# Storing x^T by blocks of three tiles instead of tile by tile, with new order numbers, in a fused attention and softplus-MLP kernel

## The chip, the cores and the metric

The kernel runs on one core of a Trainium2 chip. The metric is the device time of one execution in microseconds (us). A profile is one such execution, recorded by the hardware profiler; its span runs from the first to the last instruction.

## What is computed

The reference takes q, k and v (8 batches, 8 heads, 576 rows, 64 columns), a gain g_norm and two weights. Linear attention, a root-mean-square norm per head, and a two-layer MLP with a softplus between follow:

```python
kv  = np.einsum('bhsd,bhse->bhde', k, v)
out = np.einsum('bhsd,bhde->bhse', q, kv)
x   = out / sqrt(mean(out * out, axis=-1) + 1e-6) * g_norm     # 4608 rows of 512 after the heads are joined
h   = x @ w_in                                                  # 512 x 2048
y   = (maximum(h, 0) + log1p(exp(-abs(h)))) @ w_out             # 2048 x 512
```

The weights come as 64-bit floats and are put together from their words on the core; each factor of the MLP is split into parts (three for x and the weights), so a product is several TensorE passes.

## The kernel before

**Tiles, blocks and phases.** The 4608 rows of x are 36 tiles of 128 rows (P). Three tiles (TB) make a block of 384 rows (NT); there are 12 blocks. The 2048 hidden columns are 16 chunks of 128. The MLP goes in three phases over the chunks (`ENDS`): in phase 0 blocks 0 to 3 take four chunks each and the others six, in phases 1 and 2 the rest. One pair of block and chunk is a step, 192 in all. A step (`step`, lines 647 to 695) is twelve matmuls of x with w_in (L660, 128x384), softplus and its splitting on ScalarE (L682, L684) and VectorE (L671, L675), and nine matmuls with w_out (L667). At a phase's end the partial sums go to DRAM (L724) and come back in the next (L707).

**The attention part** (`rows`, from line 508) makes one tile of x after the other. q is turned, by TensorE (L577) and a copy on ScalarE (L584) for batches 0 and 1, by VectorE (L552) for the later ones, whose q is loaded by `load_q` in eight transfers a batch. TensorE multiplies with kv (L521) into one of two PSUM slots `o`. ScalarE squares (L590), VectorE sums by head (L525), GpSimd takes the root (L528, L529), VectorE multiplies (L533). `kv_of` loads k and v (L491, and L489 for the last rows of a batch) and forms kv on TensorE (L502) in a PSUM slot: s0 or s1 for the first two batches, the single slot `tp` for the rest.

**x^T.** The MLP needs x turned. For the first twelve tiles (`BY_PE`) TensorE turns it (`turn_x`, L539) into a PSUM slot `xp`: the slot `tp` for tiles 0 to 5 (`AT_ONCE`), an `o` slot for tiles 6 to 11. Tiles 0 to 5 are split straight from PSUM for phase 0 (`split`, L445 on ScalarE, L448 and L452 on VectorE). All twelve are also copied by ScalarE (L599) into a slot of ring m, and stored into the DRAM array xd (L600), 256 KB a tile, in rows of 128 floats (512 bytes). Tiles from 12 on are turned by VectorE (L616) into the buffer xb, and a block of three is stored by four transfers (L620). `x_again` (L635) loads a tile of x^T back, again in rows of 512 bytes (L638), in phase 0 for tiles from 6 on and in the later phases for all, and splits it; it waits for the stores listed in `x_there`.

**Weights.** `weight` loads a chunk of w_in or w_out (L283, 512 KB) into one of two raw slots, puts the floats together (L294 to L324) and `divide` splits them (L356 to L378).

**Order.** Every operation is a task with an engine, a cost in ns, the tasks it follows, the slots it takes (`take`) and gives back (`give`), and a position `pos`. The planner (`Plan.order`, line 69) runs through a simulated time when the kernel is built: among tasks of an engine that could start within 150 ns of one another, the lowest `pos` goes first. A task whose slot is not free is passed over. A task with a `size` books the transfer engines for so many ns, and its end is 2000 ns later. The order is fixed by that; on the chip each engine takes its instructions in it, and each waits for what it needs. SyncE (SP) issues nearly all transfers, in order. Ring m has 13 slots (four of them kept from loads), xb and tp have one, o has two. Where TensorE has time free early on, the planner puts in spare matmuls of the identity (`warm`, L778), up to the seventh step.

**Positions.** The list P0 gives them: CONVERT when the first four chunks' factors are converted, FETCH when they are loaded, EARLY the attention part's offsets, LATER the other chunks' factors. EARLY[0] and [1] set the tiles of block 0: tile t stands at `t * EARLY[0] + EARLY[1]`. EARLY[5] sets kv of batch 0 ahead of tile 0, EARLY[9] and [10] how far ahead of their use the loads of x^T and of partial sums are listed.

Of the kernel before, what the change touches and what calls it, by code (L numbers as in the profile page):

```python
# [18 lines left out]
P = 128  # L19
# [21 lines left out]
class Plan:  # L41
# [15 lines left out]
    def slot(self, ring):  # L57
        return Slot(ring)

    def add(self, engine, ns, run, after=(), pos=0.0, take=(), give=(), size=0, behind=None, follows=None):  # L60
        t = Task(engine, ns, run, [a for a in after if a is not None], pos, list(take), list(give), size)
        for s in t.give:
            s.readers += 1
        self.tasks.append(t)
        t.follows = follows
        t.behind = behind
        return t
# [79 lines left out]
def kernel(  # L147
# [24 lines left out]
    nc = tc.nc  # L172
# [5 lines left out]
    KD, KF = d_model // P, d_ff // P  # L178
    NT = 384
    TB = NT // P  # L180
# [6 lines left out]
    PLACES = 8  # L187
    LAST = PHASES[-1]

    P0 = [-72.5, -3.2, -24.8, -9.7, -19.6, 1.5, -23.9, 2.2, -63.0, -49.3, -55.7, -21.2, -38.7, -7.7,  # L190
          -2.7, -4.7, 2.0, -26.5, 14.0, 10.5, 5.5, 17.5, -2.0, 2.5, 3.5, 21.5, -35.0, 10.0, 6.5, 41.0,
          51.0, 65.5, 53.5, 72.5, 90.5, 95.5, 114.5, 109.5, 111.5, 8.5]
    CONVERT, FETCH, EARLY, LATER = P0[:8], P0[8:16], P0[16:27], P0[27:]
    BY_PE = 12
    AT_ONCE = 2 * TB
# [27 lines left out]
    slot, add = plan.slot, plan.add  # L223

    def new(s, shape, dtype=F32):
        if s.ring == "o":
            s.tile = o_banks[:, :, s.place]
            return s.tile
        pool = ps if s.ring in PS else sb
        s.tile = pool.tile(shape, dtype, tag=f"{s.ring}_{s.place}", name=f"{s.ring}_{s.place}")  # L230
        return s.tile
# [172 lines left out]
    xd = [dram.tile([d_model, NT], F32, name=f"x{n}") for n in range(n_blocks)]  # L404
    xb_slots = {}
    x_there = {}
# [26 lines left out]
    def split(ph, t, x, ready, pos):  # L433
        n, i = divmod(t, TB)
        if i == 0:
            xv_slots[ph, n] = slot("xv")
        dst = xv_slots[ph, n]

        def cols(m, dtype=F32):
            if dst.tile is None:  # L440
                new(dst, [P, 3, KD, NT], F32R)
            return (dst.tile if dtype == F32R else dst.tile.bitcast(F32))[:, m, :, i * P:(i + 1) * P]

        def high():
            nc.scalar.activation(cols(0, F32R), x.tile, func=AF.Identity, scale=g_down)  # L445

        def low():
            nc.vector.scalar_tensor_tensor(out=cols(1, F32R), in0=x.tile, scalar=g_col, in1=cols(0),  # L448
                                           op0=ALU.mult, op1=ALU.subtract)

        def less():
            nc.vector.scalar_tensor_tensor(out=cols(2, F32R), in0=cols(1), scalar=-RADIX, in1=cols(0),  # L452
                                           op0=ALU.mult, op1=ALU.add)

        before = x_split.get((ph, n), [None])[-1:]
        a = add("ACT", 700, high, [ready] + ([] if i == 0 else [first_high[ph, n]]), pos, [dst] if i == 0 else [])
        if i == 0:
            first_high[ph, n] = a
        b = add("DVE", 740, low, [a], pos, [], [x])
        c = add("DVE", 700, less, [b], pos)  # L460
        x_split.setdefault((ph, n), []).append(c)
# [6 lines left out]
    def x_pos(t):  # L468

        n = t // TB  # L470
        return t * EARLY[0] + EARLY[1] if n == 0 else first_step[0, n] - (EARLY[2] if n == 1 else EARLY[3]) + t % TB
# [35 lines left out]

    def rows(t):
        pos = x_pos(t)
        tp, qT, o, x, r, xp, xg = (slot(n) for n in ("tp", "m", "o", "x", "r", "tp" if t < AT_ONCE else "o", "m"))  # L510

        def out_rows():

# [27 lines left out]
        def part_of_qT(n, r0):  # L541
            if qT.tile is None:
                new(qT, [P, NP, P])
            return qT.tile[:, :, r0:r0 + n]

        turned = []
        for b, r0, n, s0 in parts(t):
            if b >= 2:
                if b not in q_slots:
# [3 lines left out]
                        out=part_of_qT(n, r0),  # L553
                        in_=q_slots[b].tile.rearrange("k (p s) -> k p s", p=NP)[:, :, s0:s0 + n]),
# [24 lines left out]
            tp = turn_q.__defaults__[-1]  # L579
# [3 lines left out]
            a = add("PE", 440, turn_q, [ld], pos - 1, [tp], [q_s])  # L583
# [3 lines left out]
        a = o_task = add("PE", 640, out_rows, turned + need, pos, [o], [qT])  # L587
        for pt in parts(t):
            o_tasks.setdefault(pt[0], []).append(a)
        a = add("ACT", 600, lambda: nc.scalar.activation(new(x, [P, H, D]).rearrange("s (a k) d -> s a (k d)", k=2), o.tile, func=AF.Square,  # L590
                                                              scale=D ** -0.5), [a], pos, [x])
        a = add("DVE", 690, reduce, [a], pos, [r])
        a = add("POOL", 2300, root, [a], pos)
        a = add("DVE", 700, norm, [a, o_task], pos, [], [o, r])
        if t < BY_PE:
            a = add("PE", 440, turn_x, [a], pos + 0.5, [xp], [x])
            if t < AT_ONCE:
                split(0, t, xp, a, pos + 0.5)
            a = add("ACT", 600, lambda: nc.scalar.copy(new(xg, [P, KD, P]), xp.tile), [a], pos + 1, [xg], [xp])  # L599
            x_there[t] = [add("SP", 450, lambda: nc.sync.dma_start(  # L600
                out=x_of(t), in_=xg.tile), [a], pos + 1, [], [xg], 1000)]
            return


# [1 line left out]
        n, i = divmod(t, TB)  # L606
        g = TB if n < n_blocks - 1 else 1
        i0, i = i - i % g, i % g
        if i == 0:
            xb_slots[n] = slot("xb"), []  # L610
        xb, turns = xb_slots[n]
# [18 lines left out]
    def x_of(t):  # L630

        n, i = divmod(t, TB)
        return xd[n][:, i * P:(i + 1) * P].rearrange("(a p) t -> p a t", p=P)
# [120 lines left out]
    for c in range(KF):  # L754
        for j in (2 * c, 2 * c + 1):
            pos = CONVERT[j] if c < 4 else LATER[c - 4] + LATER[12] * (j % 2)
            weight(j, pos, FETCH[j] if c < 4 else pos)
    for b in range(B):
        kv_of(b)
        for t in range(n_tiles):  # L760
            if parts(t)[-1][0] == b:
                rows(t)
# [51 lines left out]
```

## Time and profile before

| | |
|---|---|
| three runs | 908.24, 908.87, 909.06 us |
| median | 908.87 us |
| the profiled execution | 908.87 us |
| its span | 907.1 us |
| mean granted TensorE clock | 0.996 |
| first product of the MLP (L660) starts | 39.67 us |
| last product (L667) ends | 903.2 us |
| the twelve stores of x^T (L600) are issued | 29.4 to 95.4 us |
| bytes moved | 131.59 MB in 211,835 packets |

A row of groups has the line, the engine, the operation, its output and input tiles, its shape and count, then busy us, the mean ns of one, and the idle time of the engine ahead of it with what ended it. "PEld" is the load of the stationary operand, "SPq" the queue of SyncE. In the line of slices each digit is the busy share of a fortieth of the span (22.7 us) in tenths, 9 being 90% or more.

### The profile page before, as it was taken

How to read it: one execution, taken by the hardware profiler on the slowest of the kernel's cores; microseconds unless marked ns; L12 is line 12 of the kernel's file. 1: busy time of each engine (PE TensorE's matmuls, PEld its weight loads, DVE VectorE, ACT ScalarE, POOL GpSimd, SP SyncE). 2: the span in 40 equal slices, each digit the busy share in tenths (PEclk: the TensorE clock that was granted, in tenths of full speed). 3: DMA queues.
4: the chain of work that ended last, by engine and by line, in shares of the span. 5: the costliest groups of instructions: out<-in, count | busy, mean ns of one | idle time of the engine just before them, and what ended most of it. 6: DMA issues, size and time to landing. Idle time of an engine off the chain costs nothing.

```text
span 907.1 us, 15612 instructions
## 1 busy us (share of the span) xinstructions
PE 894.2 (99%) x5984; PEld 789.1 (87%) x5984; DVE 624.6 (69%) x1054; ACT 409.9 (45%) x788; POOL 82.8 (9%) x79
## 2 busy tenths in 40 slices
PE   7999999999999999999999999999999999999998
PEld 5777888888888899998998999989999998999987
DVE  6977988676577877788677778886534555555553
ACT  4766555343444556644445444554323333333331
POOL 0433322122213200000000000000000000000000
PEclk8999999999999999999999999999999999999999
DMA  9999988579672626355344446550330433433323
GB/s 245 267 210 281 249 172 227 134 164 182 188 152 50 161 94 186 105 187 162 105 128 128 139 148 182 194 187 22 105 103 2 140 105 88 122 105 104 105 71 105
DMA packets 211835, 131.59 MB, mean 145 GB/s; under 512 B 102704, under 2 KB 185648, under 8 KB 211760
## 3 DMA queue, kind: packets, MB, share of 16 engines
q1 hardware_dynamic: 211600, 130.59, 52.8%
q8 instruction: 47, 0.77, 0.4%
q14 instruction: 28, 0.23, 0.1%
q10 hardware_dynamic: 160, 0.00, 0.0%
HBM read 91.75 MB, written 38.80 MB: 144 GB/s over the span
## 4 chain that ended last, share of the span: by engine, by line
PE 95%; DMA 3%; ACT 1%; DVE 0%; issue 0%; SPq 0%
PE h L660 44%; PE s L667 44%; DMA m<-in_v_dram 2%; PE o_banks L521 2%; PE tp L502 2%; PE h L778 1%; PE s L502 1%; PE tp L577 0%; DMA x<-m 0%; ACT m L599 0%; DVE xv L448 0%; PE tp L539 0%; PE o_banks L539 0%; PE h L374 0%; ACT m L584 0%
## 5 line engine op out<-in xcount | busy, mean ns | idle before, releaser
L660 PE MATMUL h<-xv,w 128*128 128x384 f32 x2304 | 434.8, 337 | 0.2 <-ACT w L378 0.2
L667 PE MATMUL s<-w,gv 128*128 128x512 f32 x1728 | 433.9, 395 | 0.0
L660 PEld LDWEIGHTS h<-xv,w 128*128 128x128 f32 x2304 | 406.4, 188 | 16.4 <-ACT w L378 0.7
L667 PEld LDWEIGHTS s<-w,gv 128*128 128x128 f32 x1728 | 319.6, 188 | 60.8 <-DVE gv L675 0.2
L682 ACT ACTIVATE g<-h 128x384 f32<-128x384 f32 x192 | 94.4, 492 | 399.2 <-PE h L660 397.1
L671 DVE TENSOR_TENSOR gv<-g,gv 128x384 fp32r<-128x384 f32 x192 | 106.5, 555 | 174.5 <-ACT gv L684 173.7
L684 ACT ACTIVATE gv<-g 128x384 fp32r<-128x384 f32 x192 | 100.8, 525 | 27.9 <-PE s L667 19.7
L675 DVE SCALAR_TENSOR_TENSOR gv<-gv 128x384 fp32r<-128x384 f32 x192 | 106.7, 556 | 5.6
L448 DVE SCALAR_TENSOR_TENSOR xv<-m,g_col,xv 128x512 fp32r<-128x512 f32 x102 | 75.9, 744 | 0.6 <-ACT xv L445 0.6
L452 DVE SCALAR_TENSOR_TENSOR xv<-xv 128x512 fp32r<-128x512 f32 x108 | 74.3, 688 | 2.7
L445 ACT ACTIVATE xv<-m,g_down 128x512 fp32r<-128x512 f32 x102 | 70.1, 711 | 2.2 <-DMA m<-x 2.0
L529 POOL TENSOR_TENSOR r<-r,half 128x8 f32<-128x8 f32 x36 | 65.3, 1813 | 3.0
L709 DVE SCALAR_TENSOR_TENSOR m<-s,scale,m 128x512 f32<-128x512 f32 x24 | 17.9, 746 | 29.7 <-PE s L667 29.7
L528 POOL TENSOR_SCALAR r<-r 128x8 f32<-128x8 f32 x36 | 16.5, 459 | 219.1 <-DVE r L525 218.6
L533 DVE TENSOR_TENSOR x<-o_banks,r 128x512 f32<-128x512 f32 x36 | 24.8, 688 | 15.3 <-POOL r L529 10.1
L709 DVE SCALAR_TENSOR_TENSOR m<-s,m 128x512 f32<-128x512 f32 x36 | 23.8, 685 | 12.4 <-PE s L667 12.3
L359 DVE TENSOR_TENSOR m<-m,w 128x512 f32<-128x512 f32 x30 | 20.5, 687 | 14.2 <-ACT w L356 14.1
L521 PEld LDWEIGHTS o_banks<-kv,m 64*64 64x64 f32 x1152 | 19.9, 134 | 10.7 <-issue 4.7
L311 ACT ACTIVATE sq<-sq,big 128x512 bf16<-128x512 bf16 x32 | 22.9, 716 | 11.0 <-DVE m L307 11.0
L525 DVE TENSOR_REDUCE r<-x 128x8 f32<-128x512 f32 x36 | 24.3, 679 | 5.0 <-ACT x L590 4.7
L521 PE MATMUL o_banks<-kv,m 64*64 64x64 f32 x1152 | 24.6, 224 | 1.2 <-ACT m L584 0.7
L590 ACT ACTIVATE x<-o_banks 128x512 f32<-128x512 f32 x36 | 21.2, 594 | 7.6 <-PE o_banks L521 3.9
(71 smaller groups left out, 429.1 us busy)
## 6 DMA issues: line engine op xcount, KB each, us to landing
m<-x SPq DMA_DIRECT2D x102, 256.0 KB, 4.7
part<-m SPq DMA_DIRECT2D x72, 256.0 KB, 2.3
m<-part SPq DMA_DIRECT2D x72, 256.0 KB, 4.0
raw<-in_moe_w_in_dram SPq DMA_DIRECT2D x16, 512.0 KB, 5.7
m<-in_k_dram SPq DMA_DIRECT2D x32, 256.0 KB, 4.8
m<-in_v_dram SPq DMA_DIRECT2D x32, 256.0 KB, 4.6
raw<-in_moe_w_out_dram SPq DMA_DIRECT2D x16, 512.0 KB, 5.5
qa<-in_q_dram SPq DMA_DIRECT2D x48, 144.0 KB, 4.7
```

Of the source, the lines that this page charges most:

```text
L445: nc.scalar.activation(cols(0, F32R), x.tile, func=AF.Identity, scale=g_down)
L448: nc.vector.scalar_tensor_tensor(out=cols(1, F32R), in0=x.tile, scalar=g_col, in1=cols(0), op0=ALU.mult, op1=ALU.subtract)
L452: nc.vector.scalar_tensor_tensor(out=cols(2, F32R), in0=cols(1), scalar=-RADIX, in1=cols(0), op0=ALU.mult, op1=ALU.add)
L521: nc.tensor.matmul(y[r0:r0 + P // 2, a, c0:c0 + D], lhsT=qT.tile[e * D:(e + 1) * D, p, r0:r0 + P // 2], rhs=kvs[b % 2][e * D:(e + 1) * D, ...
L529: nc.gpsimd.tensor_tensor(out=r.tile, in0=r.tile, in1=half, op=ALU.pow)
L660: nc.tensor.matmul(hp, lhsT=w_in.tile[:, i, kd * P:(kd + 1) * P], rhs=xv.tile[:, i, kd], start=(m == 0), stop=(m == 3 * KD - 1))
L667: nc.tensor.matmul(mine[i].tile, lhsT=gv.tile[:, m, i * P:(i + 1) * P], rhs=w_out.tile[:, m], start=(c == cs[0] and m == 0), stop=(c == cs ...
L671: nc.vector.tensor_tensor(out=gv.tile[:, 1], in0=g.tile, in1=gv.tile.bitcast(F32)[:, 0], op=ALU.subtract)
L675: nc.vector.scalar_tensor_tensor(out=gv.tile[:, 2], in0=f32[:, 1], scalar=-RADIX, in1=f32[:, 0], op0=ALU.mult, op1=ALU.add)
L682: a = add("ACT", 490, lambda: nc.scalar.activation(new(g, [P, NT]), h.tile, func=AF.Softplus, scale=1.0 + E), [a], s, [g], [h])
L684: a = add("ACT", 530, lambda: nc.scalar.activation(new(gv, [P, 3, NT], F32R)[:, 0], g.tile, func=AF.Copy, scale=DOWN), [a], s, [gv])
L709: a = add("DVE", 700, lambda: nc.vector.scalar_tensor_tensor(out=new(ot, [P, d_model]), in0=bank.tile, scalar=(scale if ph == LAST else 1. ...
```

## The change

The numbers of P0 differ, and the tail of `rows` for the first twelve tiles: ScalarE copies a tile not into a slot of ring m of its own but into its third of a block's buffer xb, the single buffer that blocks 4 to 11 use. The first tile of a block takes xb; the third is followed by one transfer of the whole block, 768 KB, whose rows are 384 floats (1536 bytes) on both sides, and whose end gives xb back. `x_there` of all three tiles is that one store. The three copies are kept in the order of the tiles' lines (`follows`). In `load_q` nothing differs: it had eight transfers a batch before.

```diff
-    P0 = [-72.5, -3.2, -24.8, -9.7, -19.6, 1.5, -23.9, 2.2, -63.0, -49.3, -55.7, -21.2, -38.7, -7.7,
-          -2.7, -4.7, 2.0, -26.5, 14.0, 10.5, 5.5, 17.5, -2.0, 2.5, 3.5, 21.5, -35.0, 10.0, 6.5, 41.0,
-          51.0, 65.5, 53.5, 72.5, 90.5, 95.5, 114.5, 109.5, 111.5, 8.5]
+    P0 = [-74.0, 0.3, -15.3, -11.7, -11.1, 1.5, -22.9, 2.2, -78.5, -42.8, -76.2, -17.2, -26.2, -5.2,
+          -0.2, -4.2, 1.5, -19.5, 14.0, 10.5, 5.5, 25.5, -2.0, 2.5, 3.5, 2.5, -45.5, 7.5, 6.5, 38.5,
+          52.0, 65.5, 54.5, 72.5, 91.0, 94.5, 114.5, 110.5, 111.0, 8.5]
     CONVERT, FETCH, EARLY, LATER = P0[:8], P0[8:16], P0[16:27], P0[27:]
...
-            a = add("ACT", 600, lambda: nc.scalar.copy(new(xg, [P, KD, P]), xp.tile), [a], pos + 1, [xg], [xp])
-            x_there[t] = [add("SP", 450, lambda: nc.sync.dma_start(
-                out=x_of(t), in_=xg.tile), [a], pos + 1, [], [xg], 1000)]
+
+            n, i = divmod(t, TB)
+            if i == 0:
+                xb_slots[n] = slot("xb"), []
+            xb, turns = xb_slots[n]
+
+            def copy():
+                if i == 0:
+                    new(xb, [P, KD, NT])
+                nc.scalar.copy(xb.tile[:, :, i * P:(i + 1) * P], xp.tile)
+
+            turns.append(add("ACT", 600, copy, [a], pos + 1, [] if i else [xb], [xp], follows=turns[-1] if turns else None))
+            if i == TB - 1:
+                st = add("SP", 450, lambda: nc.sync.dma_start(
+                    out=xd[n].rearrange("(a p) t -> p a t", p=P), in_=xb.tile), turns, pos + 1, [], [xb], 2280)
+                for u in range(t - i, t + 1):
+                    x_there[u] = [st]
             return
```

More of the change, by code (lines that the diff above doesn't have):

```diff
@@ L509, in rows @@
         pos = x_pos(t)
-        tp, qT, o, x, r, xp, xg = (slot(n) for n in ("tp", "m", "o", "x", "r", "tp" if t < AT_ONCE else "o", "m"))
+        tp, qT, o, x, r, xp = (slot(n) for n in ("tp", "m", "o", "x", "r", "tp" if t < AT_ONCE else "o"))
         def out_rows():
```

## The prediction

> **What bounds the kernel now.** I read the page first: busy shares and slices, then TensorE's order of work, then the chain of waits, then what the DMA engines do in the stretch where TensorE loses time.
>
> ```profile
> span 907.1 us, 15612 instructions
> ...
> PE 894.2 (99%) x5984; PEld 789.1 (87%) x5984; DVE 624.6 (69%) x1054; ACT 409.9 (45%) x788; POOL 82.8 (9%) x79
> ...
> PE   7999999999999999999999999999999999999998
> ...
> DMA  9999988579672626355344446550330433433323
> ```
>
> TensorE is the bound: busy 894.2 of 907.1 us. But busy is not useful. The groups of TensorE hold the spare matmuls of L778, which only fill gaps:
>
> ```profile
> L778 PE MATMUL h<-ident_r 128*128 128x512 f32 x54 | 20.4, 497 | 1.6 <-DVE ident_r L746 1.6
> ...
> L502 PE MATMUL s<-m,m 128*64 128x64 f32 x128 | 6.4, 250 | 4.3 <-DMA m<-in_v_dram 4.1
> ```
>
> So 20.4 us of spare work and 12.9 us idle (907.1 less 894.2) are all that any change of order or transfers can win; the other 874 us are products that the change leaves alone. TensorE's timeline shows where they lie (start, length, idle before it):
>
> ```profile
> 1.61 4.76 PE L778 MATMUL h<-ident_r 128*128 128x512 f32 x12 [1.61 <-DVE ident_r L746]
> ...
> 39.67 2.35 PE L660 MATMUL h<-xv,w 128*128 128x384 f32 x12
> ...
> 57.72 1.06 PE L778 MATMUL h<-ident_r 128*128 128x512 f32 x3
> ...
> 66.43 0.69 PE L502 MATMUL tp<-m,m 128*64 128x64 f32 x16 [0.94 <-DMA m<-in_v_dram]
> ```
>
> The first step's product starts at 39.67. Behind it only seven spare matmuls stand (0.40 + 1.06 + 0.71 + 0.40 = 2.6 us) and idle times of 0.21, 0.22, 0.94, 0.42 and 0.31 (2.1 us): 4.7 us lost between 39.67 and 90. Some 3.9 us of idle time are the end of the span, after the last product. The rest, about 24 us, is lost ahead of 39.67. From 90 to 903 TensorE doesn't wait at all.
>
> In that first stretch the transfers set the pace. A table by stretch (TensorE, weight loads, VectorE, ScalarE, GpSimd, granted clock, DMA share, GB/s) reads:
>
> ```profile
> 20.00:30.00 10.00, 9.48 (x166) 6.68 (x162) 9.05 (x16) 8.63 (x18) 4.32 (x4) 1.00 1.00 275
> ...
> 70.00:80.00 10.00, 9.58 (x119) 7.38 (x117) 8.00 (x14) 6.32 (x12) 1.96 (x3) 1.00 1.12 315
> ...
> 200.00:300.00 100.00, 100.00 (x934) 86.33 (x934) 65.12 (x111) 42.53 (x82) 22.64 (x20) 1.00 0.66 152
> ```
>
> DMA is at 0.9 to 1.1 up to 100 us, and VectorE at about 9 of 10 from 20 to 60: two near-bounds at once. Later DMA has a third of its time free, so a saved transfer there is worth nothing.
>
> **The stores (lines 599 to 601).** Twelve stores of 256 KB become four of 768 KB.
>
> ```profile
> L600 SPq DMA_DIRECT2D x<-m x12: 360/374/734, 29.4 to 95.4; - x12
> ...
> DMA to landing us min/median/max: 2.5/4.6/6.6
> ```
>
> All twelve lie in the saturated stretch. *Packets.* In the trace's packet records a 512-byte packet takes 28 to 32 ns in the stretches up to 100 us, a 1024-byte one 53 to 56, a 2048-byte one 87 to 92. The trace before has no 1536-byte packet: not under 54 ns, not over three of 29 (87 ns); I take 73, the middle of the rows for 1024 and 2048, which stand on both sides. A block is now 1536 packets x 29 / 16 engines = 2.78 us and becomes 512 x 73 / 16 = 2.34: 0.45 us saved (0 to 1.05), 1.8 us for four blocks (0 to 4.2). Block 3's store comes at about 95, when TensorE no longer loses time, so 1.35 us of it count (0 to 3.2). It can only eat into the 4.7 us lost after 39.67, whose largest pieces wait for loads (the value tiles at 66.43; w_in of the fourth chunk, which lands at 52.30 and holds the fourth step until 61.93). I take it whole: **-1.4 us**.
>
> The Trainium skill has a rule that speaks against this term: "DMA: Bandwidth & Descriptors", section "Specifications", has transfers from 512 bytes on at line rate, so that longer rows would win nothing. This trace differs: 512 bytes in 29 ns are 17.7 bytes per ns, 2048 in 92 are 22.3. By the page the term would be 0 and the forecast 908.0.
>
> *SP.* Eight issues fewer, 8 x 0.374 = 3.0 us of SP's time. At nothing: transfers land 4 to 7 us after their issue though each needs about 1 us of the engines, so SP is ahead by a backlog. SP's waits for the copies (6.7 us in six waits, the longest 2.4) are under that backlog too. If it were gone, each wait would stop the loads behind it, up to 2.4 us.
>
> **The ring m.** Each of the twelve copies held one of 13 slots from copy to landing, about 0.6 + 4.6 + 0.4 us; 12 x 5.6 = 67 slot-us over 70 us, so one slot in 13 comes free. The trace shows once what it cost: ScalarE's L599 waits 0.86 us at 88.15 for an earlier store, and the chain of waits runs through it. I take half, **-0.4 us** (0 to -0.9).
>
> **The numbers P0.** No transfer or instruction is added, all are re-ordered. Up to 22 us the loads keep their sequence: the same two factors first, then batch 0 of k and v, w_out of chunk 0 when a raw slot is free, then q. What moves is conversion: w_in of chunk 1 (-24.8 to -15.3) falls behind the first three tiles (-26.5, -24.5, -22.5 become -19.5, -18.0, -16.5). Tile 2's norm (L533) starts at 35.53 although GpSimd had finished at 34.42, its reduction at 31.10 although ScalarE had finished at 29.57: 1.1 + 1.5 us. But the instructions in front of both are mostly the splits and the norm of tiles 0 and 1, not conversions, so little of it can go: gain up to 2.6, loss up to the price of the second rival below (4). I take **-0.5**, near the gain that the rows leave. The retimed loads of x^T and partial sums (21.5 to 2.5, -35.0 to -45.5) matter only after the steps they are tied to; DMA's free third from 200 us on hides them, and without that cover one late load costs a TensorE step's wait of 1 to 2 us.
>
> **The wait that is added.** A block's x^T can only be stored after its third copy, and the next block can only be copied when xb is free. Reads: block 2's third copy ends at 79.6. A tile's store there landed in 3.7 us; two more tiles' worth of data (2 x 0.8) make it 5.3: 84.9. The reads then land at about 89 to 91.4, the last split (0.71 + 0.75 + 0.69) ends at about 94. Before it ended at 94.2, and the ninth step's product began at 96.7: margin 2.4 us, so **0**. If the block store takes the longest landing, 6.6 + 1.6 = 8.2 us, 0.5 us is lost. Block 3: reads from 99.5 instead of 95.9, step 12 at 115.5 against a last split at 112.2; behind the third rows that margin is 3.3 against 3.6 us of delay, 0.3 us at worst. Queued behind a waiting read on SP are k and v of later batches, whose products have no due time that TensorE misses there.
>
> **Sum.** -1.4 - 0.4 - 0.5 = -2.3. The profiled execution took 908.87 us, 1.8 us more than its span, and is the median of the three runs itself: 908.9 - 2.3 = **906.6**.
>
> **Rivals.** *First, slower: the single buffer xb.* Look at the copies of tiles 6 and 5 on ScalarE, and the first turn into xb on VectorE:
>
> ```profile
> 66.02 0.58 ACT L599 COPY m<-o_banks 128x512 f32<-128x512 f32 x1
> ...
> 70.45 0.58 ACT L599 COPY m<-tp 128x512 f32<-128x512 f32 x1
> ```
>
> Tile 6 (block 2) is copied before tile 5 (block 1). With one xb it must wait for block 1's store: 71.1 + 5.3 + 1.6 = 78.0, twelve us later, and holds one of two o banks meanwhile. Tile 8's output rows, at 77.2 before, slip past 78.6, its copy to about 81.5, block 2's splits to about 97 and beyond. The price is what passes the margin: about 2 to 4 us with the waits behind it on ScalarE, if the new order doesn't bring tile 5 forward; likewise the first turn of block 4 (96.25) meets block 3's store, which lands at about 99.5: 3.2 us on VectorE, with the splits of g queued behind. It decides from a wait of over 2.4 us. For it: VectorE and ScalarE are in order. Against: the planner counts xb as taken and places work in the gap. About 911.9. Chance 0.20.
>
> *Second, slower: the weights come late.* Conversion of chunk 1 behind the tiles is six instructions on VectorE (0.43 + 0.69 + 0.69 + 0.43 + 0.69 + 0.69 = 3.6 us) and one of 0.69; the second step starts at 44.43, 4.8 us after the first, so the work fits only just. If it comes wholly behind the tiles, TensorE fills up with spare matmuls for up to 4 us: about 911.5. Chance 0.15.
>
> *Third, no difference:* the saving and the margin eat one another, or DMA isn't what TensorE waits for, since VectorE at 9 of 10 is as near a bound; 908.5. Chance 0.27. That the change doesn't do what it says: the loads of q are already eight a batch (48 of 144 KB), so that half brings nothing; and a row could be cut into pieces, though the trace moves 4096-byte rows whole. Both end here.
>
> **How the numbers follow.** Faster by over 0.2% (about what a measurement of this kernel can tell from no change): 0.38, my forecast. Within: 0.27. Slower: 0.20 + 0.15 = 0.35. Low end: packets at their best (-3.2), all the delay of tile 2 (-2.6), the whole m wait (-0.9) make 902.2. High end: the two waits of the first rival's upper price with a part of the second's, 913.5. The forecast's own range is 902.2 to 907.0.
>
> **What would show it.** Right: four stores of about 2.3 us of engine time, 1536-byte packets near 73 ns, the first L660 at 38 to 40 us, fewer than seven spare matmuls after it, no wait of ScalarE at the copies. Wrong: idle time on ScalarE at the copies or on VectorE at L616 put down to x<-xb, spare matmuls between the first two steps, the ninth step past 97. What would upset it most is the new order, which no row of the profile before shows.

## The result and the profile after

The changed kernel takes 912.26 us (median of four runs, 911.27 to 913.10) beside 908.94 before: a ratio of 1.0038, with an interval from 1.0020 to 1.0055. It is slower by 3.3 us where 2.3 us less was forecast. Ten more runs in a later session gave 911.45, 1.0028 (1.0016 to 1.0040). The profiled execution took 911.85, its span 910.1.

The same lines of the page as before:

```profile
span 910.1 us, 15578 instructions
...
PE 894.0 (98%) x5982; PEld 788.3 (87%) x5982; DVE 625.8 (69%) x1054; ACT 409.6 (45%) x788; POOL 83.0 (9%) x79
...
PE   7899999999999999999999999999999999999998
...
DMA  9999979489682535355344435651330433433323
```

TensorE's busy time is the same within 0.2 us, so the 3.0 us of span are idle time: 910.1 less 894.0 are 16.1 us, 12.9 before. TensorE's groups name what ended it:

```profile
L521 PE MATMUL o_banks<-kv,m 64*64 64x64 f32 x1152 | 24.6, 224 | 2.4 <-DVE x L533 0.9 <-ACT xb L608 0.7 <-ACT m L584 0.5
L792 PE MATMUL h<-ident_r 128*128 128x512 f32 x52 | 20.1, 509 | 1.6 <-DVE ident_r L760 1.6
...
L502 PE MATMUL s<-m,m 128*64 128x64 f32 x128 | 5.9, 237 | 5.7 <-DMA m<-in_v_dram 5.5
```

The spare work is as large as it was (20.1 for 20.4 us). The waits for the value tiles of the first kv products (L502, into s) have grown from 4.1 to 5.5 us. New is a wait of 0.7 us for the copy into xb (L608) and one of 0.9 for a norm (L533). These two stand just ahead of the ninth step, in TensorE's timeline:

```profile
98.95 0.60 PE L539 MATMUL o_banks<-ident_r,x 128*128 128x128 f32 x4
100.22 0.69 PE L521 MATMUL o_banks<-kv,m 64*64 64x64 f32 x32 [0.68 <-ACT xb L608]
100.85 0.69 PE L502 MATMUL tp<-m,m 128*64 128x64 f32 x16
102.43 0.69 PE L521 MATMUL o_banks<-kv,m 64*64 64x64 f32 x32 [0.90 <-DVE x L533]
103.05 2.36 PE L674 MATMUL h<-xv,w 128*128 128x384 f32 x12
```

The last line is step 9, block 2's first, at 103.05 instead of 96.7. With no product to do, TensorE goes from one attention task to the next, and these wait for one another through the two o banks. SP's issues show why block 2 is late:

```profile
85.34 0.46 SPq L612 DMA_DIRECT2D x<-xb  x1
85.85 5.12 SPq L423 DMA_DIRECT2D qa<-in_q_dram  x4
91.08 2.12 SPq L652 DMA_DIRECT2D m<-x  x3
```

Block 2's store is issued at 85.34 (its third copy began at 82.94), lands at 90.27, and its three reads follow at 91.08; before, the first two were issued at 74.78 and 81.97. They land 5.4 to 5.8 us later, at 96.7 to 98.5.

I add up TensorE's lost time (each spare matmul from its start to the next start, and idle time) from the matmul records of each profile, by stretch. The total runs to the last product and takes in the 1.6 us ahead of the first matmul, which stand in none of the three stretches:

| us lost | 0 to 40 | 40 to 80 | 80 to 120 | total |
|---|---|---|---|---|
| before | 22.4 | 4.2 | 0.3 | 28.6 |
| after | 24.4 | 3.5 | 1.9 | 31.4 |
| after's order, 512-byte rows | 22.8 | 4.3 | 1.9 | 30.6 |

The 1.6 us that are added at 80 to 120 are the same in both profiles of the new order. The 2 us ahead of 40 are in one only. A split at the first product of the MLP, instead of at 40 us, shows more; it comes behind the experiments.

### The profile page after: what moved, and what is told of

Read it like the earlier page. It is cut to its first block, busy times and chain, and to the rows that moved or that the text cites. A ratio compares the mean times of both kernels' runs of the same rounds, so it can differ in the third digit from the quotient of the medians.

```text
span 910.1 us, 15578 instructions
## 1 busy us (share of the span) xinstructions
PE 894.0 (98%) x5982; PEld 788.3 (87%) x5982; DVE 625.8 (69%) x1054; ACT 409.6 (45%) x788; POOL 83.0 (9%) x79
## 4 chain that ended last, share of the span: by engine, by line
PE 94%; DMA 3%; DVE 1%; ACT 1%; SPq 0%; issue 0%; DVEq 0%
PE h L674 45%; PE s L681 45%; PE o_banks L521 2%; PE tp L502 2%; DMA m<-in_q_dram 1%; DMA m<-in_v_dram 1%; DMA tail<-in_k_dram 1%; DMA qa<-in_q_dram 1%; DMA raw<-in_moe_w_in_dram 0%; SPq L567 0%; PE o_banks L539 0%; DVE x L533 0%; PE tp L539 0%; ACT x L590 0%; PE o_banks L577 0%
## 5 line engine op out<-in xcount | busy, mean ns | idle before, releaser
L533 DVE TENSOR_TENSOR x<-o_banks,r 128x512 f32<-128x512 f32 x36 | 24.7, 686 | 15.1 <-POOL r L529 6.5
L521 PEld LDWEIGHTS o_banks<-kv,m 64*64 64x64 f32 x1152 | 19.9, 134 | 11.5 <-issue 5.8
L525 DVE TENSOR_REDUCE r<-x 128x8 f32<-128x512 f32 x36 | 24.3, 680 | 6.6 <-ACT x L590 6.2
L521 PE MATMUL o_banks<-kv,m 64*64 64x64 f32 x1152 | 24.6, 224 | 2.4 <-DVE x L533 0.9
```

The costliest lines, as they stand in the source:

```text
L521: nc.tensor.matmul(y[r0:r0 + P // 2, a, c0:c0 + D], lhsT=qT.tile[e * D:(e + 1) * D, p, r0:r0 + P // 2], rhs=kvs[b % 2][e * D:(e + 1) * D, ...
```

## The experiments

Ratios are to the kernel before, measured in the same session. Two kinds of run must be kept apart: those in which the planner makes a new order, and those in which every instruction keeps its place, but for a few that are named.

**First, the parts of the change with the planner.** New numbers alone (`P0` of the changed kernel, all else as before):

> The stores tile by tile as before, with the new numbers P0 alone. Theory A (the loss is the new numbers: w_in of the fourth chunk is issued about 7 us later and k, v of batch 1 land 3 us later): slower by about as much as the whole change, 911 to 913 us. Theory B (the loss is the storing by blocks and what it does to the planned order, the new numbers are fitted to it): about 909 or, since the numbers don't fit the old stores, a little over, under 910.5 us. The changed kernel is at 912.3, before at 908.9.

Measured: 916.35 us, 1.0077 (1.0060 to 1.0094). Blocks alone (changed kernel, `P0` of before):

> The stores by blocks with the old numbers P0. Theory A: the loss is gone, 907 to 909.5 us. Theory B: the loss stays, 911 us or more, with the ninth step's product (block 2's first) starting past 97 us, since its reads of x^T are issued behind the store of the whole block.

Measured: 913.50, 1.0051 (1.0027 to 1.0075). Each part alone is slower than before and, by the medians, slower than both together, so neither of the two theories in the expectations (A, the numbers; B, the blocks) holds as put. Part of these two times is a halved clock, of which the last section tells. But block stores with the old numbers show the same waits ahead of step 9 as the changed kernel (0.7 us for the copy into xb, 0.9 for the norm). In the chain of waits of this run the read of x^T stands between TensorE's instructions:

```profile
92.14 0.53 PE o_banks L539 x4
92.68 5.00 DMA m<-x
97.68 0.02 issue
97.70 0.73 ACT xv L445
```

Step 9 starts at 104.48 there. Next, the changed kernel with a store for each tile out of xb:

```diff
-            if i == TB - 1:
-                st = add("SP", 450, lambda: nc.sync.dma_start(
-                    out=xd[n].rearrange("(a p) t -> p a t", p=P), in_=xb.tile), turns, pos + 1, [], [xb], 2280)
...
+            x_there[t] = [add("SP", 450, lambda: nc.sync.dma_start(
+                out=x_of(t), in_=xb.tile[:, :, i * P:(i + 1) * P]), [turns[-1]], pos + 1, [], [xb], 1000)]
```

> Changed kernel, but each tile is stored by itself from its third of xb as soon as it is copied (512-byte rows, 256 KB), and its read waits for that store alone. The single buffer xb stays. If the wait for a block's third copy costs the 1.6 us that TensorE idles at 100 to 103 us: reads of block 2 from about 83 instead of 91 us, ninth step at 95 to 98 us, total about 910.5 us. If the single buffer costs it: no better, 912 us. If the order of the first loads costs the most (2 us ahead of the first product): that part stays unless the planner's order of k, v and w_out changes too.

Measured: 918.03, 1.0092 (1.0075 to 1.0109), the worst of all. The planner made another order, in which TensorE stands 4.14 us for tile 11's norm:

```profile
105.60 0.72 PE L539 MATMUL o_banks<-ident_r,x 128*128 128x128 f32 x4 [4.14 <-DVE x L533]
```

So this run says nothing on the wait for a block: the new order hides it. Then the row length, in the changed kernel's own order (one task issues three transfers):

```diff
+                def store():
+                    for u in range(TB):
+                        nc.sync.dma_start(out=x_of(t - i + u), in_=xb.tile[:, :, u * P:(u + 1) * P])
```

> Changed kernel with every instruction in the same planned order, only the store of a block is issued as three transfers of 256 KB in rows of 512 bytes instead of one of 768 KB in rows of 1536. Packets: 1536 x 29 ns / 16 = 2.8 us for a block instead of 512 x 75 / 16 = 2.4. If the row length matters as the prediction's first term had it: slower by up to 1.4 us, 913.6 us. If TensorE doesn't wait for those transfers, or the reads of the first tiles, which then wait for a third alone, gain as much: 912.3 us, no change.

Measured: 913.12, 1.0038 (1.0023 to 1.0053): no difference from the changed kernel that these intervals (0.15% either way) can show. The profile does show one. Block 1's last part lands at 75.07, ScalarE waits 1.33 us for it with tiles 6 and 7, and TensorE waits 0.88 us for their copy:

```profile
75.17 1.07 ACT L608 COPY xb<-o_banks 128x512 f32<-128x512 f32 x2 [1.33 <-DMA x<-xb]
...
76.30 1.16 PE L521 MATMUL o_banks<-kv,m 64*64 64x64 f32 x64 [0.88 <-ACT xb L608]
```

None of the three profiles of this order with 1536-byte rows has that wait. In the one that starts as early (first product at 39.62 against 39.70, one load moved, see below) the block's store is issued at 67.57, as the first of the three is here (67.66), and lands at 72.50. So in that order too one transfer with longer rows is worth 0.9 us of TensorE's time, by way of the single buffer.

**Second, how much a new order alone moves the time.** Kernel before, the booked 1000 ns of a store (L601) replaced by 760 and by 900; same instructions, same `P0`:

```diff
-                out=x_of(t), in_=xg.tile), [a], pos + 1, [], [xg], 1000)]
+                out=x_of(t), in_=xg.tile), [a], pos + 1, [], [xg], 760)]
```

> The kernel before, with the same transfers, copies and numbers P0; only the transfer time that the planner books for a store of x^T is 760 ns instead of 1000 (a third of the block store's 2280), so the planner makes another order. If the numbers P0 are fitted to one order and any other loses (theory C): slower by 1 to 8 us like the other new orders, 910 to 917 us. If only the block store or only the new P0 does harm: no change, 908.5 to 910 us.

Measured: 913.24, 1.0042 (1.0027 to 1.0057).

> A second neutral change of the planner's books: the kernel before with 900 ns instead of 1000 for a store of x^T, nothing else. Theory C: slower by 1 to 8 us. Otherwise no change. The two together say how much the time moves when only the order is made anew.

Measured: 909.66, 1.0004 (0.9994 to 1.0013). One number in the planner's books that is no work at all can cost as much as the whole change, or nothing. (Most of the 760 ns run's loss is a halved clock, see the last section; its one execution with a mean clock of at least 0.995 took 910.63, 0.2% over before.) A comparison across orders is therefore no measure of the stores. The same with the changed kernel (2400 for 2280):

> The changed kernel with only the booked transfer time of a block store at 2400 ns instead of 2280. If the new numbers P0 are fitted to the changed kernel's order as the old ones are to theirs, another order loses against 912.3 us: 912.5 to 917. If the changed kernel's order is no better than any other: as likely below 912.3 as above it.

Measured: 911.84, 1.0032 (1.0020 to 1.0044), no different from the changed kernel: this one neighbour gives no sign that its numbers are at a sharp best.

**Third, block stores in the order of before.** The tasks, their places and the slots they book stay; blocks 0 and 1, read back only in phase 1, go through buffers in weight slots that are filled much later:

```diff
+            def copy():
+                if n > 1:
+                    nc.scalar.copy(new(xg, [P, KD, P]), xp.tile)
+                    return
+                if i == 0:
+                    xb_slots[n] = sb.tile([P, KD, NT], F32, tag=f"w{1 - n}_7_0", name=f"w{1 - n}_7_0")
+                nc.scalar.copy(xb_slots[n][:, :, i * P:(i + 1) * P], xp.tile)
...
+                elif i == TB - 1:
+                    nc.sync.dma_start(out=xd[n].rearrange("(a p) t -> p a t", p=P), in_=xb_slots[n])
```

> The kernel before with every instruction in its planned order and the old numbers; only blocks 0 and 1, whose x^T is read back much later, are copied into a block's buffer (of their own, in weight slots filled later) and stored by one 768 KB transfer at the place of the third tile's store. So nothing waits for the block and nothing is re-ordered. If longer rows and fewer stores are worth something by themselves: 0.9 us less (two blocks at 0.45), about 908.3 with before at 909.2. If they are worth nothing here and the loss comes from the new order and the added wait (my theory now): no change, within 0.5 us of before.

Measured: 907.98 beside 909.02, 0.9991 (0.9982 to 1.0000): 0.8 us by the ratio, beside the 0.9 us of the forecast's packets, at the edge of what can be told. The same with 512-byte rows (three transfers for the one):

> As the run with blocks 0 and 1 by block in the order of before, but the block goes out as three transfers of 512-byte rows at the place of the third tile's store. If that run's gain (0.8 us) is the longer rows: gone, 909.0. If it comes from the first two stores of a block being put off behind more urgent loads: kept, about 908.0.

Measured: 909.60, 1.0011 (1.0002 to 1.0020). The intervals of the two don't overlap: in this order 1536-byte rows in one transfer are worth 0.2% against three transfers of 512-byte rows. (Row length and the number of issues differ together. Both runs put the whole block at the place of its third tile's store; against before, which spreads the stores, the gain is the 0.1% above.) Where it shows is one line. With 512-byte rows a value tile is late:

```profile
79.05 0.69 PE L502 MATMUL tp<-m,m 128*64 128x64 f32 x16 [1.08 <-DMA m<-in_v_dram]
```

With 1536-byte rows the same instruction doesn't wait:

```profile
77.27 0.66 PE L539 MATMUL o_banks<-ident_r,x 128*128 128x128 f32 x4
77.85 0.69 PE L502 MATMUL tp<-m,m 128*64 128x64 f32 x16
```

Now block 3 as well (`n not in (0, 1, 3)` for `n > 1`), whose reads stood behind its last store already:

> As the kernel before in its order, with blocks 0, 1 and 3 stored by block; block 2 goes tile by tile, nothing is moved. SP then stands at block 3's first read until the store has landed, about 4 us with loads of w_in, k and v behind it. If that is covered: 907.5 to 908 us, the gain of blocks 0 and 1 or a little more. If SP's wait costs: 909 us or more, with idle time of TensorE between 105 and 125 us.

Measured: 908.72, 1.0000 (0.9991 to 1.0009). SP's first read of block 3 is issued at 98.58 instead of about 96, TensorE has no idle time after it, and nothing is won either. And all four, tiles 6 and 7 read and split behind block 2's store:

```diff
+    move([again[0, 6], again[0, 7]], again[0, 8])
+    move(splits[0, 6] + splits[0, 7], splits[0, 8][0])
```

> The order of the kernel before, all four blocks stored by block from buffers of their own; the reads of tiles 6 and 7 and their splits are moved behind to those of tile 8, so that they come after block 2's store, nothing else is moved. If the wait for a whole block costs TensorE 1.6 us by itself: block 2's step (the ninth) starts at about 98 to 103 us instead of 96.7 and the time is 0.5 to 2 us above that of blocks 0 and 1 alone (907.98 beside 909.02), so 909 to 910. If the wait is covered, as the prediction had it with a margin of 2.4 us: about 907.5, and the loss of the changed kernel was that of its order alone.

Measured: 910.17, 1.0019 (1.0010 to 1.0028); against blocks 0, 1 and 3 that is 1.0019 - 1.0000 = 0.2% (1.7 us by the ratios, 1.5 by the medians) for block 2's wait. TensorE has one gap more than with two blocks:

```profile
90.95 2.25 PE L690 MATMUL s<-w,gv 128*128 128x512 f32 x9
94.99 0.63 PE L540 MATMUL o_banks<-ident_r,x 128*128 128x128 f32 x4 [1.79 <-DVE x L534]
```

It waits for a norm (L534 here), and VectorE's timeline shows what stands in front of that norm:

```profile
90.12 0.75 DVE L448 SCALAR_TENSOR_TENSOR xv<-w,g_col,xv 128x512 fp32r<-128x512 f32 x1 [1.34 <-ACT xv L445]
90.91 0.69 DVE L452 SCALAR_TENSOR_TENSOR xv<-xv 128x512 fp32r<-128x512 f32 x1
91.52 0.74 DVE L448 SCALAR_TENSOR_TENSOR xv<-w,g_col,xv 128x512 fp32r<-128x512 f32 x1
92.30 0.69 DVE L452 SCALAR_TENSOR_TENSOR xv<-xv 128x512 fp32r<-128x512 f32 x1
...
94.16 0.68 DVE L534 TENSOR_TENSOR x<-o_banks,r 128x512 f32<-128x512 f32 x1
```

The splits of tiles 6 and 7, which were spread over 82 to 91 us, come in one bunch when the block's store has landed, ahead of the norm that TensorE's next task needs. Here the wait for a block isn't paid where the data is read, but by what is queued behind the late splits on VectorE. (Where exactly they were put is my choice in this run.)

The changed kernel with a buffer for each block:

```diff
-                xb_slots[n] = slot("xb"), []
+                xb_slots[n] = slot(("w1_7", "w0_7", "w1_6", "w0_6")[n]), []
```

> The changed kernel, but each of the four blocks has a buffer of its own (weight slots that are filled much later) instead of the one xb, so that no copy has to wait for the store of the block before. In the changed kernel tile 6 is turned into an o bank at 65.3 us and copied only at 75.0, when block 1's store has landed; for these 9.7 us TensorE has one o bank, and no output rows start between 60.2 and 76.6. If the single buffer is what makes block 2 late: tile 6's copy within 2 us of its turning, output rows of tile 8 near 68 us, block 2's third copy near 80 instead of 83.5, step 9 at 98 to 100 instead of 103, total 909.5 to 911. If the wait for the whole block is all: step 9 at 103 and 912 us. As the planner makes a new order, the places say more than the total.

Measured: 910.87, 1.0026 (1.0016 to 1.0036). All the places came as expected, or earlier, if the single buffer is what makes block 2 late. In the changed kernel the o banks take one turned tile at 65.25 and the next output rows only at 76.60, two tiles at once:

```profile
60.22 0.69 PE L521 MATMUL o_banks<-kv,m 64*64 64x64 f32 x32
65.25 0.66 PE L539 MATMUL o_banks<-ident_r,x 128*128 128x128 f32 x4
...
71.02 0.66 PE L539 MATMUL o_banks<-ident_r,x 128*128 128x128 f32 x4 [0.48 <-DVE x L533]
76.60 1.16 PE L521 MATMUL o_banks<-kv,m 64*64 64x64 f32 x64
```

With own buffers the next output rows follow at 66.40 (in before at 68.55), and two more sets start at 73.17 and 79.39:

```profile
64.54 0.66 PE L539 MATMUL o_banks<-ident_r,x 128*128 128x128 f32 x4
66.40 0.69 PE L521 MATMUL o_banks<-kv,m 64*64 64x64 f32 x32
...
73.17 0.69 PE L521 MATMUL o_banks<-kv,m 64*64 64x64 f32 x32
```

In the changed kernel tile 6 (with tile 7) is copied only here, on ScalarE:

```profile
74.98 1.06 ACT L608 COPY xb<-o_banks 128x512 f32<-128x512 f32 x2
```

With own buffers tile 6's copy runs at 65.72 instead of 74.98, block 2's third at 77.24 instead of 82.94, step 9 starts at 97.29 instead of 103.05, and TensorE idles 0.1 us at 80 to 120 instead of 1.9. Yet the time falls by 0.6 to 1.4 us only, and the intervals overlap. Blocks 2 and 3 tile by tile again, with the new numbers, say the same:

```diff
+            if n > 1:
+                a = add("ACT", 600, lambda: nc.scalar.copy(new(xg, [P, KD, P]), xp.tile), [a], pos + 1, [xg], [xp])
+                x_there[t] = [add("SP", 450, lambda: nc.sync.dma_start(
+                    out=x_of(t), in_=xg.tile), [a], pos + 1, [], [xg], 1000)]
+                return
```

> The changed kernel with its new numbers, but blocks 2 and 3, which are read back in phase 0, go tile by tile through ring m again; blocks 0 and 1 are stored by block. If block 2's late reads cost the 1.6 us of TensorE's idle time at 100 to 103 us: that idle time goes, the ninth step starts at about 97 us, total 910.5 us. If any new order loses more than that (theory C): 911 to 917 us in spite of an earlier ninth step.

Measured: 911.68, 1.0026 (1.0017 to 1.0035). Step 9 starts at 98.77 and the idle time at 80 to 120 is gone, but a new idle time of 0.84 us stands at 123, again ahead of output rows (L521); the time hardly moves. The same rows and transfers in the old order are 0.9991 (blocks 0 and 1 have buffers of their own there, and share xb here): the order that the planner makes of the new numbers costs 0.35% (3.2 us) here.

**Fourth, what of the new order costs, and how far the idea goes.** The changed kernel with one load moved (the fetch and the first square of w_out's chunk 2), and the changed kernel again:

```diff
+    behind(fetches[5], max(kv_loads[1, 3], key=done.index))
+    behind(squares[5], copies[2])
```

> The changed kernel in its order, with one load moved: w_out of chunk 2 (512 KB), which stands ahead of the last k and v of batch 1 in the new order, goes behind them, and ScalarE's first instruction on it behind tile 2's copy. If those late k and v (v lands at 38.75 us instead of 35.83, TensorE waits 1.3 us for it) cost the end of the kernel time: 1 to 1.5 us below the changed kernel in the same job. If the time lost ahead of 40 us is caught up by the next wait for loads, as two profiles of the same order with first products at 39.7 and 40.9 us suggest: no change.

> The changed kernel as it is, for a second profile of the same order and for a comparison on the same chip with the run that moves one load: 911.5 to 912.5 us, the first product anywhere from 39.5 to 41 us, the idle times of 0.7 and 0.9 us at 100 to 103 us there again.

Measured: 911.88 (1.0033, 1.0023 to 1.0043) with the load moved, 911.45 (1.0028) without: no gain in the medians, although in its profile the wait of 1.31 us for the last v of batch 1 is gone and the first product starts at 39.62. That doesn't make the time ahead of the first product harmless. The changed kernel's order has three profiles here, with the first product at 39.62 (load moved), 40.93 and 42.83, and in each the last product ends 865.2 to 865.3 us later: a late start is not caught up. The start differs from execution to execution, and that this load makes it earlier doesn't show in the medians. And both stores of blocks 0 and 1 put off to 94 us, in the old order:

```diff
+    for t in (2, 5):
+        done.remove(x_there[t][0])
+        done.insert(done.index(x_there[11][0]) + 1, x_there[t][0])
```

> The order of the kernel before, blocks 0 and 1 stored by block (768 KB, 1536-byte rows) from buffers of their own, and both stores put off until after the last tile's store at 95 us, past the stretch in which the transfers are saturated; nothing reads them before phase 1. If transfer time in that stretch is what TensorE waits for: up to 2 us below before, 907 us, less than with the stores in place (907.98 against 909.02). If 0.8 us was all that could be won: 908.

Measured: 907.41 beside 908.90, 0.9984 (0.9976 to 0.9993). This version beats both kernels; against the stores in place (0.9991) it is better by the medians alone, for the intervals overlap. The stores stand behind TensorE's last wait, although the transfers are still busy there (DMA share 1.03 at 80 to 100 us, 1.05 at 100 to 120):

```profile
L613 SPq DMA_DIRECT2D x<-w x2: 507/522/537, 93.9 to 94.4; - x2
```

**The lost time split at the first product.** Behind the first product TensorE's lost time is the same, to 0.01 us, in every profile of one order with the same rows; ahead of it executions of one order differ. From the matmul records, added up as in the table above:

| us lost | ahead of the first product | behind it |
|---|---|---|
| before | 24.0 | 4.6 |
| old order, blocks 0 and 1 / and block 3 / stores late | 24.1 / 24.3 / 23.7 | 3.6 / 3.6 / 3.6 |
| old order, blocks 0 and 1, 512-byte rows | 24.2 | 4.7 |
| old order, all four blocks | 24.3 | 5.4 |
| changed kernel / again / load moved | 26.0 / 27.0 / 24.8 | 5.4 / 5.4 / 5.4 |
| its order, 512-byte rows | 24.4 | 6.2 |
| new numbers, own buffers | 25.1 | 4.6 |
| new numbers, blocks 0 and 1 only | 24.2 | 5.6 |

Behind the first product block stores win 0.9 us (blocks 0 and 1) or nothing (block 3) and cost 1.8 (block 2). The changed kernel loses 0.8 more than before, and without the single buffer it loses no more than before. Ahead of it the four profiles in the changed kernel's order have 25.6 us on the mean, the six in the order of before 24.1: 1.5 us more, from one execution each.

## Why the prediction was wrong

**The bound and where time is to be won:** right. The products cost the same where the clock isn't halved; what moves is the time lost up to 125 us.

**The stores, -1.4 us:** right in mechanism, too large for this kernel. A 1536-byte packet takes 66 to 91 ns by stretch, 75 and 66 for blocks 0 and 1 (73 taken). In an unchanged order two blocks bring 0.8 us where 0.9 was worked out, by the wait that the forecast named, a late value tile (0.94 us at 66.43). That the numbers agree is luck: blocks 0 and 1, with block 3 added, or stored late all leave the same 3.6 us behind the first product. The gain is that one wait, and once it is gone more saved transfer time wins nothing there; the forecast took packet time for TensorE's time, and the seven spare matmuls, the rest of its 4.7 us, stand in all these runs. In the changed kernel's order the rows are worth 0.9 us in the profile, at the copy into the single buffer, and too little to show in the medians.

**The wait that is added, 0 us:** this step failed. Behind the first product the wait for block 2 costs 1.8 us in the old order (5.4 against 3.6), and the single buffer 0.7 with the new numbers (5.4 against 4.6 with own buffers, in an order planned for them). "Block 2's third copy ends at 79.6" took the old times of the copies as given, but the copies move, this one to 83.5: with one xb, tile 6 is copied at 74.98, right after block 1's store has landed at 74.61, and holds an o bank from 65.25 on. That is the first rival, in its place (tile 6's copy, worked out at 78.0) and with its consequence (output rows of later tiles slip, step 9 past 97): without the single buffer it is gone. What the forecast held against the rival came true and didn't help: the planner places other work in the gap, so ScalarE shows no wait at the copies, but the bank is held all the same, and the copy keeps its planned place even when the store lands earlier (at 72.50 with one load moved, the copy at 73.68). That the rival's 911.9 is near the measured time is in part luck, for own buffers win back only 0.6 to 1.4 us of it. (The step at 115.5, which the forecast calls the twelfth, is the thirteenth, block 3's first.) And even with the copies in place (run with all four blocks in the old order: store issued at 78.46, reads landing at 87.3 to 89.7, much as worked out) the block costs those 1.8 us, since I set the arrival of x^T against the next product alone and not against VectorE's queue.

**P0, -0.5 us:** this step failed too, and in its sign. I priced the moved conversions one by one, but a new order is a new order as a whole: neutral changes of one booked number gave +0.04% and +0.42%. The stretch was the right one: ahead of the first product the new order loses about 1.5 us more by the profiles, within the bounds (a gain of 2.6, a loss of 4), and what is lost there is not caught up. But it isn't the conversions that show. In the changed kernel's profile 1.4 of the 1.9 us of added idle time there (8.7 for 6.8 us) are waits for value tiles, though the forecast had the loads keep their sequence up to 22 us and looked no further. The second rival's spare matmuls between the first steps did not appear: steps 1 to 3 start at 40.9, 45.2 and 48.1, 4.3 and 2.9 us apart.

**The ring m, -0.4 us:** not tested by itself. The wait for an m slot at 88 us is gone in the profile after, and others took its place.

**The sum:** in the old order block stores with own buffers cost +0.19% in all, -0.09% for the rows and the rest for the waits. The changed kernel is at +0.38% and +0.28% in its two sessions, 2.5 to 3.3 us. Of these 0.8 us is lost behind the first product: 1.6 us of idle time at 100 to 103 us that the single buffer causes, less what the changed order saves at 40 to 80 us. About 1.5 us is lost ahead of it, by profiles that scatter by 2.6 us; it is an indication and no proof. Where the single buffer is taken away with the new numbers kept, +0.26% remain, so most of the loss goes with the new order. Which task of that order makes it stays open; the one load of w_out ahead of the last k and v of batch 1 is not enough to explain it.

## What to carry to other kernels

Before you merge transfers, ask who reads them back and when: the merge wins where the data lies for long (blocks 0 and 1), and only as much as the one wait that it removes; it loses where a reader waits for the last part, because the readers' work then comes in one bunch, ahead of other work in the planned order of VectorE. A single buffer that is held until a long store lands also holds whatever waits to be copied into it, here one of two PSUM banks. When a planner makes the order, change one thing in a fixed order first; compare the stretches of a profile that repeat from one execution to the next; and run neutral changes of its books, for a re-ordering alone can move the time more than the change does.

## What was not expected of the hardware

Some new orders lose more time than their idle and spare time shows. The kernel with 760 ns booked has a total of 29.4 us lost, 0.9 more than before, yet its span is 4.3 us longer. Its table by stretch shows the granted clock (the number ahead of the DMA share) at 0.84 in the middle of useful work:

```profile
40.00:60.00 20.00, 17.94 (x202) 13.88 (x203) 16.06 (x28) 13.56 (x27) 6.44 (x6) 0.99 1.00 235
60.00:80.00 20.00, 19.95 (x240) 15.93 (x241) 14.28 (x24) 10.44 (x20) 6.48 (x6) 0.84 0.90 214
```

The clock was halved for 6.8 us from 59.5 on, after gaps of TensorE of 0.54 and 0.95 us among spare matmuls:

```profile
57.89 1.06 PE L778 MATMUL h<-ident_r 128*128 128x512 f32 x3 [0.54 <-ACT g L682]
59.89 1.12 PE L577 MATMUL o_banks<-ident_r,m 128*128 128x128 f32 x4 [0.95 <-DVE x L533]
```

The second profile of the changed kernel has it at 34.6 to 41.4 us (after waits of 1.0 and 1.9 us), the run with new numbers alone at 119.6 (in a wait of 3.5), the store for each tile at 106.0 (after the wait of 4.1), blocks with old numbers at 103.6 (after 0.7 and 0.9). Every profile also has a halved stretch of 3.4 or 6.8 us ahead of 18 us; before and the runs in its order have no other up to the last product. But the changed kernel's first profile has gaps of 0.7 and 0.9 at 100 to 103 and no halving after them. The Trainium skill, "TensorE: Matmul & The Clock Gate", section "HAM oscillation — how this bites in real kernels", gives the rule that idle gaps of TensorE should stay under about 3.4 us. The halvings at waits of 3.5 and 4.1 us agree with it, the other three don't: in these runs gaps of 0.5 to 1.9 us, a few close together, went ahead of a halving in some executions and not in others; what decides isn't shown.

How often it comes can be counted. The stretch ahead of 18 us (half of at most 6.8 us in 907) and one behind the last product take under 0.005 of the mean clock in every profile, so an execution with a mean under 0.995 has another. Of the executions of before that ran beside the experiments 4 of 112 have one, of the changed kernel 1 of 14, but of the four kernels new numbers alone, blocks with old numbers, a store for each tile and 760 ns booked 20 of 24. The changed kernel's loss is therefore not the clock; theirs is in part (the two executions of blocks with old numbers that have none took 910.58 and 911.34).
